# The statistics of the first four tiles of a fused block, shared out anew between VectorE, ScalarE and GpSimd

## The chip, the core and the metric

The kernel runs on one core of one Trainium2 chip. The metric is the device time of one execution in microseconds; the median of seven runs of the kernel before is 174.38 us.

## What is computed

The input x has 2048 rows (tokens) of 448 columns. It is normalized once, and two branches work on the normalized rows: an attention with a softmax feature map, and a token-shifting MLP. The sum of x and both branches is the output.

```
def _layernorm(x, eps=1e-5):
    m = mean(x, axis=-1); v = var(x, axis=-1)
    return (x - m) / sqrt(v + eps)

xn = _layernorm(x)
# A: qkv = xn @ wqkv; phi = softmax feature map of q, k by w_phi; linear attention; @ wo
# B: h = gelu(_layernorm(xn) @ w1), shifted by tokens in four groups of columns, @ w2; x1 = xn + that
#    x1 + gelu(_layernorm(x1) @ w3) @ w4
out = x + A(xn) + B(xn)
```

The change concerns only the first line of that, the normalization of x, and of it only the first four of sixteen tiles.

## The kernel before

**Tiles.** A tile is 128 rows. `xtok` holds the sixteen tiles of x, `xn` the normalized ones in 512 columns, `xnT` their transposes, which nearly all matmuls read. Per tile, `st`, `mv` and `rs` hold eight float32 columns each: raw statistics, mean and variance, and the reciprocal root.

**Who sets the order.** The order is written out by hand. A recorder keeps the instructions in program order; each engine runs its own in that order, and a semaphore is waited for wherever a tile was written by another engine. So an instruction that waits holds up everything behind it on its engine. `play` runs a list of steps that stand in the wanted order.

**Loads.** The loads are issued at the start. SyncE's queue has tile 0, tile 2, tile 3, the second half of `wv`, tiles 4 and 5, tiles 6 and 7, `w1`, then the rest; ScalarE's queue has tile 1 and the first half of `wv`, and then loads an activation table.

**Head, tiles 0 to 3.** `ln1_two(i)` does two tiles: for each, VectorE takes the statistics (`ln_stats`: a statistics instruction over 448 columns and an aggregate that gives mean and variance), and ScalarE takes the square root of variance plus epsilon (`epsb` holds the epsilon); then for each, VectorE takes the reciprocal and applies mean and factor (`ln1_apply`, one instruction over 512 columns with the two halves overlapping). It is called for tiles 0 and 1, and then for 2 and 3. From tile 4 on, `ln1_stats` does the statistics on VectorE and lets GpSimd add epsilon and raise to the power of -1/2 (`ln_scale`, with `mhalf` holding -0.5).

`xn_T(i, b)` transposes a tile by eight TensorE instructions into the bank pair b, from where ScalarE copies it into `xnT` (from tile 10 on in part VectorE). `spin(n, 256)` is n matmuls on dummy data, which keep TensorE busy while it waits.

**The first matmuls.** `V(i, 0)` and `V(i, 1)` are the two parts of `v_pair(i, b)`, the product of tiles i and i + 1 with `wv`, eight matmuls and six; `row_pairs` issues them in pairs, one on the lower and one on the upper 64 partitions. `WA` and `WC` are products with `w1`, `FO` folds `w_phi` into the query and key weights, `v_out` copies a V result out of the bank (ScalarE). The list begins:

```
ln1_two(0)
spin(19, 256)
play([(xn_T, 0, 0), (spin, 3, 256), (xn_T, 1, 1)])
ln1_two(2)
...
play([(spin, 4, 256), V(0, 0), (xn_T, 2, 0), V(0, 1), (xn_T, 3, 1),
      (spin, 2, 256), V(2, 0), (v_out, 0, 2), (tables, "gelu_apprx_tanh_and_others"), WA(0, 0), (xn_T, 4, 1),
      V(2, 1), (v_out, 2, 3), (xn_T, 5, 2), WA(0, 1), WC(0, 0), (xn_T, 6, 3), WC(0, 1), (wc_out, 0, 1),
```

ScalarE has the table with the square root loaded at first, and the one with the gelu between the copy of V(0) and the first gelu. Behind this stage come the folds, the attention's feature maps, the shifted product with `w2`, and the long stage of `w3`, `w4` and `wo`, all of them as before.

Of the kernel before, what the change touches and what calls it, by code (L numbers as in the profile page):

```python
# [5 lines left out]
ACT = mybir.ActivationFunctionType  # L6
ALU = mybir.AluOpType
AX = mybir.AxisListType
BF16 = mybir.dt.bfloat16
F32 = mybir.dt.float32  # L10

LN_EPS = 1e-5
# [208 lines left out]
def bass_parallel_sum__linear_kernel_hedgehog__mixer_s_mlp__prompt_kernel(  # L221
    nc, A_x, A_wqkv, A_w_phi, A_wo, B_x, B_w1, B_w2, B_w3, B_w4, out,
):
    _, S, D = A_x.shape
# [3 lines left out]
    NT, NG, KC, NC, NM, FC, HP = 16, 4, 4, 4, 4, 14, 32  # L228
# [7 lines left out]
    with es:  # L236
        R = Recorder(nc, es)
        total = [0]

        def region(name, nbytes):  # L240
            nbytes = -(-nbytes // 64) * 64
            total[0] += nbytes
            h = es.enter_context(nc.sbuf_tensor(name, [128, nbytes // 2], BF16))
            R.track(h, nbytes)
            return h

        def view(h, cols, dt=BF16, at=0):
            a = h[:, at // 2:at // 2 + cols * DTB[dt] // 2]
            return a if dt == BF16 else a.bitcast(dt)

        def new(name, cols, dt=BF16):
            return view(region(name, cols * DTB[dt]), cols, dt)
# [6 lines left out]
        banks = [pairs[b // 2][:, 512 * (b % 2):512 * (b % 2) + 512] for b in range(8)]  # L259


        xtok = new("xtok", NT * D).rearrange("p (t d) -> p t d", t=NT)
        xn = new("xn", NT * 512).rearrange("p (t d) -> p t d", t=NT)
        xnT_r = region("xnT", KC * S * 2)
        xnT = view(xnT_r, KC * S).rearrange("p (c s) -> p c s", c=KC)
# [11 lines left out]
        wv = new("wv", KC * D).rearrange("p (c d) -> p c d", c=KC)  # L277
# [20 lines left out]
        st = new("st", NT * 8, F32).rearrange("p (t c) -> p t c", t=NT)  # L298
        mv = new("mv", NT * 8, F32).rearrange("p (t c) -> p t c", t=NT)
        rs = new("rs", NT * 8, F32).rearrange("p (t c) -> p t c", t=NT)  # L300
# [3 lines left out]
        ksum = new("ksum", 4 * 32, F32).rearrange("p (b c) -> p b c", b=4)  # L304
        rks = new("rks", 4 * 32, F32).rearrange("p (b c) -> p b c", b=4)
        mhalf = new("mhalf", 8, F32)
        epsb = new("epsb", 8, F32)

        h3T = view(phik_r, 2 * FC * 512).rearrange("p (b c f) -> p b c f", b=2, c=FC)
        oT = view(xnT_r, 2 * KC * 512).rearrange("p (b c s) -> p b c s", b=2, c=KC)  # L310
# [30 lines left out]
        dve, pool = "DVE", "POOL"  # L341
# [43 lines left out]
        def tables(name):  # L385
            R.op("ACT", lambda e: e.preload_act_table_set(name), [], [])

        tables("sqrt_and_others")
        R.ew(pool, "memset", ident[:, :], 0.0)
        R.op(pool, lambda e: e.affine_select(ident[:, :], ident[:, :], pattern=[[-1, 128]],  # L390
                                             compare_op=ALU.not_equal, fill=1.0, base=0, channel_multiplier=1),
# [4 lines left out]
        R.ew(pool, "memset", hD[:, :, 512:DW], 0.0)  # L396
        busy = gT[:, 0, 0, 0:256]
        R.ew(dve, "memset", busy, 1.0)
        R.ew(dve, "memset", epsb[:, :], LN_EPS)
        R.ew(dve, "memset", vp[:, :, DH + 1:HP], 0.0)  # L400
        R.ew(dve, "memset", vp[:, :, DH:DH + 1], 1.0)
        mb = maskb[0:CR, :].rearrange("p (h e) -> p h e", h=4)
# [27 lines left out]
        def lap(a):  # L430
            return bass.AP(a.tensor, a.offset, [list(a.ap[0]), [192, 2], [1, 256]])

        def halves(a):
            return a.rearrange("p (b e) -> p b e", b=2)

        def ln_stats(stt, mvt, src, i):
            R.ew(dve, "bn_stats", stt[:, i, 0:6], src[:, i, 0:D])
            R.ew(dve, "bn_aggr", mvt[:, i, 0:2], stt[:, i, 0:6])
# [8 lines left out]
        def ln_apply(eng, dst, src, mvt, rst, i):  # L447
            m, op = (mvt[:, i, 0:1], ALU.subtract) if eng == dve else (rst[:, i, 1:2], ALU.add)
            R.ew(eng, "tensor_scalar", dst, src, m, rst[:, i, 0:1], op0=op, op1=ALU.mult)
# [6 lines left out]
        def ln1_apply(eng, i):  # L456
            ln_apply(eng, halves(xn[:, i, :]), lap(xtok[:, i, :]), mv, rs, i)
# [3 lines left out]
        def spin(n, cols):  # L461
            for _ in range(n):
                R.mm(banks[7][:, 0:cols], busy[:, 0:128], busy[:, 0:cols], True, True)
# [49 lines left out]
        LO, HI = (0, 64), (64, 128)  # L513

        def row_pairs(first, second, start=False, cols=1):
            for s, (p, q) in enumerate(zip(first, second)):
                for out, lhs, rhs in (p, q) if cols == 1 else (*p, *q):
                    R.mm(out, lhs, rhs, start and s == 0, False)

        def lap_pair(outs, lhs, rhs):  # L520
            def side(k, rows, kcs):
                return [(outs[k], lhs(k, kc, *rows), rhs(k, kc, *rows)) for kc in kcs]
            return (lambda: row_pairs(side(0, LO, (0, 1, 2, 3)), side(1, HI, (0, 1, 2, 3)), True),
                    lambda: row_pairs(side(1, LO, (0, 1, 3)), side(0, HI, (0, 2, 3))))

        def k_pair(i, b):
            return lap_pair([banks[2 * b + k][:, 0:D] for k in range(2)],
                            lambda k, kc, lo, hi: xnT[lo:hi, kc, 128 * (i + k):128 * (i + k) + 128],
                            lambda k, kc, lo, hi: wpk[lo:hi, kc, :])

        def q_pair(g, c, b):
            return lap_pair([banks[2 * b + k] for k in range(2)],
                            lambda k, kc, lo, hi: wpq[lo:hi, kc, 128 * (c + k):128 * (c + k) + 128],
                            lambda k, kc, lo, hi: xnT[lo:hi, kc, 512 * g:512 * g + 512])

        def v_pair(i, b):
            return lap_pair([banks[2 * b + k][:, 0:D] for k in range(2)],
                            lambda k, kc, lo, hi: xnT[lo:hi, kc, 128 * (i + k):128 * (i + k) + 128],
                            lambda k, kc, lo, hi: wv[lo:hi, kc, :])

        def v_out(i, b, eng="ACT"):
            vd = vaug[:, i:i + 2, :].rearrange("p t (h e) -> p t h e", e=HP)[:, :, :, 0:DH]
# [237 lines left out]
        def play(fs):  # L780
            for f in fs:
                f[0](*f[1:])

        def ln1_two(i):
            for j in (i, i + 1):
                ln_stats(st, mv, xtok, j)
                R.act(rs[:, j, 1:2], mv[:, j, 1:2], ACT.Sqrt, bias=epsb[:, 0:1])
            for j in (i, i + 1):
                R.ew(dve, "reciprocal", rs[:, j, 0:1], rs[:, j, 1:2])
                ln1_apply(dve, j)  # L790

        ln1_two(0)
        spin(19, 256)
        play([(xn_T, 0, 0), (spin, 3, 256), (xn_T, 1, 1)])
        ln1_two(2)
        for i in range(4, 10):
            ln1_stats(i, 1, 0)
            if i > 4:
# [10 lines left out]
        def ln1_end():  # L809
# [5 lines left out]
            late_3()  # L815

        vps = {i: v_pair(i, b) for i, b in ((0, 2), (2, 3), (4, 2), (6, 3), (8, 2), (10, 2), (14, 3))}
        was = {g: wa_pair(g, b) for g, b in ((0, 0), (1, 0), (2, 0), (3, 3))}
        wcs = {g: wc_pair(g, b) for g, b in ((0, 1), (1, 1), (2, 0), (3, 0))}
# [3 lines left out]
        def V(i, k):  # L823
            return (vps[i][k],)

        def WA(g, k):
            return (was[g][k],)

        def WC(g, k):
            return (wcs[g][k],)  # L830
# [4 lines left out]
        def FO(t, m, k):  # L835
            return (fps[t, m][k],)

        play([(spin, 4, 256), V(0, 0), (xn_T, 2, 0), V(0, 1), (xn_T, 3, 1),
              (spin, 2, 256), V(2, 0), (v_out, 0, 2), (tables, "gelu_apprx_tanh_and_others"), WA(0, 0), (xn_T, 4, 1),
              V(2, 1), (v_out, 2, 3), (xn_T, 5, 2), WA(0, 1), WC(0, 0), (xn_T, 6, 3), WC(0, 1), (wc_out, 0, 1),  # L840
              V(4, 0), (xn_T, 7, 3), (wa_out, 0, 0), V(4, 1), (v_out, 4, 2), V(6, 0),
              WC(1, 0), V(6, 1), (v_out, 6, 3), WA(1, 0), (xn_T, 8, 2, 2), WC(1, 1), (wc_out, 1, 1), WA(1, 1), (wa_out, 1, 0),
# [19 lines left out]
        side = [12, 0, 1, 2, 3, 8, 9, 10]  # L862
        for ps in range(8):
            k, q = k_pair(2 * ps, 1), q_pair(ps // 2, 2 * (ps % 2), 0)
            w = (w2_pair if ps else v_pair)(side[ps], 2)
            if not ps:
                play([(k[0],), (w[0],), (k[1],), (k_exp, 0, 1, 0), (k_exp, 0, 1, 1), (q[0],), (w[1],), (v_out, 12, 2, "DVE"),
# [117 lines left out]
```

The softmax here doesn't subtract the row's maximum and nothing guards it: scores larger than these inputs give would overflow.

## Time and profile before

| what | value |
|---|---|
| median of 7 runs | 174.38 us (174.19 to 175.06) |
| the profiled execution's own time | 174.38 us |
| its span in the profile | 172.7 us |
| TensorE busy, share of the span | 168.7 us, 98% |
| VectorE, ScalarE, GpSimd busy | 114.3, 84.4, 88.8 us |
| first transposes (tile 0) start | 5.39 us |
| first WA matmul starts | 10.15 us |
| starts of the applies of tiles 0, 1, 2, 3 | 4.92, 5.44, 7.42, 7.94 us |
| starts of ScalarE's copies of tiles 0, 1, 2, 3 | 5.72, 6.38, 8.22, 8.92 us |
| second table load of ScalarE | 10.34 us, for 1.28 us |

The times inside are counted from the start of the span. A line of the timeline gives start, duration, engine, source line, operation, what is written and read, and the shape; a bracket at its end tells how long the engine was idle before it and who ended that. Nearly all instructions are recorded by a helper, so the source line is the helper's (L200 matmuls, L204 transposes, L208 ScalarE, L212 elementwise), and the tiles' names tell which step it is. In the profile, DVE is VectorE, ACT ScalarE, POOL GpSimd, PE TensorE, and PEld its weight loads.

### The profile page before, as it was taken

How to read it: one execution, taken by the hardware profiler on the slowest of the kernel's cores; microseconds unless marked ns; L12 is line 12 of the kernel's file. 1: busy time of each engine (PE TensorE's matmuls, PEld its weight loads, DVE VectorE, ACT ScalarE, POOL GpSimd, SP SyncE). 2: the span in 40 equal slices, each digit the busy share in tenths (PEclk: the TensorE clock that was granted, in tenths of full speed). 3: DMA queues.
4: the chain of work that ended last, by engine and by line, in shares of the span. 5: the costliest groups of instructions: out<-in, count | busy, mean ns of one | idle time of the engine just before them, and what ended most of it. 6: DMA issues, size and time to landing. Idle time of an engine off the chain costs nothing.

```text
span 172.7 us, 5218 instructions
## 1 busy us (share of the span) xinstructions
PE 168.7 (98%) x2272; PEld 91.5 (53%) x2272; DVE 114.3 (66%) x263; ACT 84.4 (49%) x99; POOL 88.8 (51%) x123
## 2 busy tenths in 40 slices
PE   7999999999999999999999999999999999999994
PEld 5565576544555554554555555545545555545553
DVE  4999975277999999976577962445417425474621
ACT  3599874988778877947225322224204222224000
POOL 3065570015789999930639389440720714522740
DMA  5995552139942011044103932034411220311331
GB/s 164 327 212 91 113 125 55 44 45 366 382 151 47 19 30 30 4 37 89 33 1 65 91 63 60 28 87 93 93 30 55 61 57 4 84 30 34 84 86 55
DMA packets 32679, 15.21 MB, mean 88 GB/s; under 512 B 23952, under 2 KB 32016, under 8 KB 32656
## 3 DMA queue, kind: packets, MB, share of 16 engines
q1 hardware_dynamic: 32096, 14.51, 36.5%
q8 instruction: 18, 0.29, 0.8%
q10 hardware_dynamic: 560, 0.37, 0.7%
q14 instruction: 5, 0.04, 0.1%
HBM read 7.14 MB, written 1.84 MB: 52 GB/s over the span
## 4 chain that ended last, share of the span: by engine, by line
PE 95%; DVE 2%; issue 1%; ACT 0%
PE bank L200 94%; PE bank L204 1%; DVE vaug L212 1%; DVE st L212 1%; ACT xnT L208 0%; DVE xn L212 0%; DVE mv L212 0%; DVE gT L212 0%; DVE rs L212 0%; DVE epsb L212 0%
## 5 line engine op out<-in xcount | busy, mean ns | idle before, releaser
L208 ACT ACTIVATE phik<-bank 128x1024 bf16<-128x1024 f32 (+1 forms) x44 | 42.3, 984 | 60.5 <-PE bank L200 60.5
L200 PE MATMUL bank<-gT,w 64*128 64x512 bf16 x392 | 50.2, 377 | 0.1
L212 DVE TENSOR_TENSOR vaug<-bank,vaug 128x464 f32<-128x464 f32 (+3 forms) x65 | 32.7, 512 | 22.5 <-PE bank L200 20.9
L200 PE MATMUL bank<-w,phik 64*128 64x448 bf16 (+3 forms) x434 | 45.2, 343 | 0.0
L212 POOL TENSOR_TENSOR xnT<-vaug 128x196 bf16<-128x196 f32 (+1 forms) x32 | 18.1, 587 | 46.6 <-DVE vaug L212 46.6
L200 PEld LDWEIGHTS bank<-w,phik 64*128 64x128 bf16 (+1 forms) x434 | 22.9, 94 | 20.3 <-issue 0.4
L212 POOL TENSOR_TENSOR phik<-phik,rks 128x1792 bf16<-128x1792 bf16 x8 | 25.6, 3214 | 10.4 <-DVE rks L212 10.3
L200 PEld LDWEIGHTS bank<-gT,w 64*128 64x128 bf16 x392 | 17.8, 94 | 17.6 <-issue 0.6
L212 POOL TENSOR_TENSOR vaug<-xn,xtok 128x448 f32<-128x448 bf16 x16 | 16.2, 1033 | 0.2 <-DVE vaug L212 0.2
L212 DVE RECIPROCAL vaug<-bank 128x16 f32<-128x16 f32 x16 | 4.1, 257 | 18.2 <-PE bank L200 18.2
L212 DVE TENSOR_REDUCE ksum<-phik 128x64 f32<-128x1792 bf16 x8 | 16.1, 2010 | 0.0
L200 PE MATMUL bank<-xnT,wpq 64*128 64x512 bf16 x112 | 14.7, 376 | 0.0
L200 PE MATMUL bank<-wv,xnT 64*128 64x448 bf16 x112 | 13.9, 351 | 0.1
L200 PE MATMUL bank<-wo,xnT 64*128 64x448 bf16 (+3 forms) x110 | 13.6, 343 | 0.0
L200 PE MATMUL bank<-xnT,w 64*128 64x512 bf16 (+2 forms) x168 | 13.4, 306 | 0.0
L200 PE MATMUL bank<-w,hT 64*128 64x448 bf16 x112 | 13.2, 349 | 0.0
L200 PE MATMUL bank<-wpk,xnT 64*128 64x448 bf16 x112 | 13.2, 349 | 0.0
L212 POOL TENSOR_TENSOR rs<-mv,mhalf 128x1 f32<-128x1 f32 (+2 forms) x16 | 10.8, 676 | 1.3
L212 DVE TENSOR_TENSOR xn<-bank,xn 128x512 bf16<-128x512 f32 (+1 forms) x16 | 9.2, 620 | 3.1 <-PE bank L200 3.1
L212 DVE BATCH_NORM_STATS2 st<-xtok 128x6 f32<-128x448 bf16 x16 | 9.8, 613 | 0.0
L212 POOL TENSOR_SCALAR mv<-mv 128x1 f32<-128x1 f32 (+2 forms) x16 | 3.8, 239 | 11.2 <-DVE mv L212 10.7
L212 POOL TENSOR_SCALAR g_tok<-xn,rs 128x512 bf16<-128x512 bf16 x12 | 9.1, 772 | 0.3
(67 smaller groups left out, 173.6 us busy)
## 6 DMA issues: line engine op xcount, KB each, us to landing
w<-in_B_w_dram SPq DMA_DIRECT2D x2, 896.0 KB, 5.8
out_dram<-vaug SPq DMA_DIRECT2D x15, 112.0 KB, 1.9
w<-in_B_w_dram SPq DMA_DIRECT2D x1, 1568.0 KB, 11.4
xtok<-in_A_x_dram SPq DMA_DIRECT2D x2, 448.0 KB, 6.3
xtok<-in_A_x_dram SPq DMA_DIRECT2D x2, 224.0 KB, 4.9
w<-in_B_w_dram SPq DMA_DIRECT2D x2, 224.0 KB, 5.1
wo<-in_A_wo_dram SPq DMA_DIRECT2D x2, 224.0 KB, 6.9
xtok<-in_A_x_dram SPq DMA_DIRECT2D x3, 112.0 KB, 2.8
```

The costliest lines, as they stand in the source:

```text
L200: self.op("PE", lambda e: e.matmul(out, lhsT, rhs, start=start, stop=stop, skip_group_check=True), [out], [lhsT, rhs], tile=self._tile(lhsT))
L204: self.op("PE", lambda e: e.transpose(out, in_, ident), [out], [in_, ident], tile=self._tile(in_))
L208: self.op("ACT", lambda e: e.activation(out, in_, func, **kw), [out], [in_] + aps)
L212: self.op(eng, lambda e: getattr(e, name)(out, *args, **kw), [out], aps)
```

## The change

The square root on ScalarE goes for tiles 0 to 3, and with it the square root table, the second table load and `epsb`; the gelu table is loaded at the start. Statistics of tiles 0, 2 and 3 stay on VectorE, which now also adds epsilon to the variance by a one-column instruction; the power of -1/2 comes from GpSimd. Tile 1's statistics come from ScalarE in two passes over its 448 columns that also add up what they write: one of x/448 (the mean) and one of x²/448. VectorE squares the mean and takes epsilon from it, GpSimd subtracts this from the mean of the squares and raises to the power. The passes write their unused columns into `xn` of tiles 15 and 14.

VectorE's order becomes: statistics of tile 0 with epsilon, squared mean of tile 1, statistics of tile 2 with epsilon, apply of tile 0, statistics of tile 3 with epsilon, applies of tiles 1, 2 and 3. GpSimd's is: power of tile 0, subtraction and power of tile 1, powers of tiles 2 and 3.

The first part of `v_pair` is split: for tiles 0 to 3, `V(i, 0)` has the four matmuls of the first two column blocks and `V(i, 2)` the four of the others, with the transposes of tile 3 between them at V(0); tile 2's transposes come ahead of V(0, 0). There are 19 + 5 + 1 + 2 spins in place of 19 + 3 + 4 + 2. After the first WA the order on TensorE is the old one.

```
-        tables("sqrt_and_others")
+        tables("gelu_apprx_tanh_and_others")
...
-        R.ew(dve, "memset", epsb[:, :], LN_EPS)
...
         def v_pair(i, b):
+            def side(k, rows, kcs):
+                lo, hi = rows
+                return [(banks[2 * b + k][:, 0:D], xnT[lo:hi, kc, 128 * (i + k):128 * (i + k) + 128], wv[lo:hi, kc, :])
+                        for kc in kcs]
+
+            def early():
+                row_pairs(side(0, LO, (0, 1)), side(1, HI, (0, 1)), True)
+                if i > 3:
+                    mid()
+
+            def mid():
+                row_pairs(side(0, LO, (2, 3)), side(1, HI, (2, 3)))
+            return early, lambda: row_pairs(side(1, LO, (0, 1, 3)), side(0, HI, (0, 2, 3))), mid
...
-        def ln1_two(i):
-            for j in (i, i + 1):
-                ln_stats(st, mv, xtok, j)
-                R.act(rs[:, j, 1:2], mv[:, j, 1:2], ACT.Sqrt, bias=epsb[:, 0:1])
-            for j in (i, i + 1):
-                R.ew(dve, "reciprocal", rs[:, j, 0:1], rs[:, j, 1:2])
-                ln1_apply(dve, j)
-
-        ln1_two(0)
+        def ln1_pow(j, at):
+            R.ew(pool, "tensor_tensor", rs[:, j, 0:1], mv[:, j, at:at + 1], mhalf[:, 0:1], op=ALU.pow)
+
+        def ln1_one(j):
+            ln_stats(st, mv, xtok, j)
+            R.ew(dve, "tensor_scalar", mv[:, j, 2:3], mv[:, j, 1:2], LN_EPS, 1.0, op0=ALU.add, op1=ALU.mult)
+            ln1_pow(j, 2)
+
+        def ln1_sum(j, func, scale, to):
+            out, in_, acc = xn[:, NT - 1 - to // 3, 0:D], xtok[:, j, :], mv[:, j, to:to + 1]
+            R.op("ACT", lambda e: e.activation(out, in_, func, scale=scale, accum_out=acc), [out, acc], [in_])
+
+        ln1_sum(1, ACT.Copy, 1.0 / D, 0)
+        ln1_sum(1, ACT.Square, D ** -0.5, 3)
+        ln1_one(0)
+        R.ew(dve, "tensor_scalar", mv[:, 1, 2:3], mv[:, 1, 0:1], mv[:, 1, 0:1], -LN_EPS, op0=ALU.mult, op1=ALU.add)
+        R.ew(pool, "tensor_tensor", mv[:, 1, 4:5], mv[:, 1, 3:4], mv[:, 1, 2:3], op=ALU.subtract)
+        ln1_pow(1, 4)
+        ln1_one(2)
+        ln1_apply(dve, 0)
+        ln1_one(3)
+        ln1_apply(dve, 1)
         spin(19, 256)
-        play([(xn_T, 0, 0), (spin, 3, 256), (xn_T, 1, 1)])
-        ln1_two(2)
+        play([(xn_T, 0, 0), (spin, 5, 256), (xn_T, 1, 1)])
+        ln1_apply(dve, 2)
+        ln1_apply(dve, 3)
...
-        play([(spin, 4, 256), V(0, 0), (xn_T, 2, 0), V(0, 1), (xn_T, 3, 1),
-              (spin, 2, 256), V(2, 0), (v_out, 0, 2), (tables, "gelu_apprx_tanh_and_others"), WA(0, 0), (xn_T, 4, 1),
+        play([(spin, 1, 256), (xn_T, 2, 0), (spin, 2, 256), V(0, 0), (xn_T, 3, 1), V(0, 2), V(0, 1),
+              V(2, 0), V(2, 2), (v_out, 0, 2), WA(0, 0), (xn_T, 4, 1),
```

More of the change, by code (lines that the diff above doesn't have):

```diff
@@ L306, in bass_parallel_sum__linear_kernel_hedgehog__mixer_s_mlp__prompt_kernel @@
         mhalf = new("mhalf", 8, F32)
-        epsb = new("epsb", 8, F32)
         h3T = view(phik_r, 2 * FC * 512).rearrange("p (b c f) -> p b c f", b=2, c=FC)
@@ L536, in v_pair @@
         def v_pair(i, b):
-            return lap_pair([banks[2 * b + k][:, 0:D] for k in range(2)],
-                            lambda k, kc, lo, hi: xnT[lo:hi, kc, 128 * (i + k):128 * (i + k) + 128],
-                            lambda k, kc, lo, hi: wv[lo:hi, kc, :])
+            def side(k, rows, kcs):
[9 more added lines that the diff above has]
+            return early, lambda: row_pairs(side(1, LO, (0, 1, 3)), side(0, HI, (0, 2, 3))), mid
         def v_out(i, b, eng="ACT"):
```

## The prediction

> **What bounds the kernel now.** First the page's busy rows and its chain.
>
> ```profile
> span 172.7 us, 5218 instructions
> PE 168.7 (98%) x2272; PEld 91.5 (53%) x2272; DVE 114.3 (66%) x263; ACT 84.4 (49%) x99; POOL 88.8 (51%) x123
> PE 95%; DVE 2%; issue 1%; ACT 0%
> ```
>
> TensorE is the bound almost throughout. The change touches no matmul of the body, so it can win or lose only by moving the moment from which TensorE runs without a gap. The chain in order of time gives that moment.
>
> ```profile
> 3.46 0.45 DVE st L212
> ...
> 4.92 0.42 DVE xn L212
> ...
> 5.39 0.29 PE bank L204 x8
> ...
> 8.92 0.61 ACT xnT L208
> ...
> 9.57 1.63 PE bank L200 x15
> ```
>
> To 5.39 us the chain is VectorE's statistics, then it alternates; its last step outside TensorE is ScalarE's copy of tile 3 at 8.92. From 9.57 on it is matmuls. I take as landmark the first WA matmul, which starts at 10.15: the same matmuls stand before it in both kernels (14 of V(0), 8 of V(2), transposes of tiles 0 to 3). VectorE's timeline gives the durations.
>
> ```profile
> 3.27 0.63 DVE L212 BATCH_NORM_STATS2 st<-xtok 128x6 f32<-128x448 bf16 x1
> 3.93 0.18 DVE L212 BATCH_NORM_AGGREGATE mv<-st 128x2 f32<-128x6 f32 x1
> 4.03 0.59 DVE L212 BATCH_NORM_STATS2 st<-xtok 128x6 f32<-128x448 bf16 x1
> 4.66 0.18 DVE L212 BATCH_NORM_AGGREGATE mv<-st 128x2 f32<-128x6 f32 x1
> 4.75 0.13 DVE L212 RECIPROCAL rs<-rs 128x1 f32<-128x1 f32 x1
> 4.92 0.41 DVE L212 TENSOR_SCALAR xn<-xtok,mv,rs 128x512 bf16<-128x512 bf16 x1
> 5.25 0.15 DVE L212 RECIPROCAL rs<-rs 128x1 f32<-128x1 f32 x1
> ```
>
> Start to start: statistics to aggregate 0.66; aggregate to an independent instruction 0.10, to one that needs it 0.18 + 0.04 = 0.22; a one-column step 0.10 to what needs nothing of it; an apply 0.33.
>
> **The change, part by part. VectorE's new order.** Starting at 3.27 as before (the landing of tile 0 decides that, so the lost epsilon memset gives nothing): statistics of tile 0 3.27, aggregate 3.93, epsilon 4.15, square of tile 1's mean 4.25, statistics of tile 2 4.35, aggregate 5.01, epsilon 5.23, apply of tile 0 5.33 (before 4.92), statistics of tile 3 5.66, aggregate 6.32, epsilon 6.54, apply of tile 1 6.64 (before 5.44), of tile 2 6.97 (7.42), of tile 3 7.30 (7.94), statistics of tile 4 at some 7.7 (8.27). One statistics step, one aggregate and four reciprocals go; four one-column steps come. VectorE leads by 0.5 us afterwards, but tile 1 is 1.2 us later, since its apply now stands behind all of tile 3's statistics.
>
> **Landing of tile 3.** That instruction also waits for a DMA. The DMA rows of the moment when it is issued (1.72), and of the three loads of one tile together:
>
> ```profile
> xtok<-in_A_x_dram SPq DMA_DIRECT2D x1, 112.0 KB, 4.2
> xtok<-in_A_x_dram SPq DMA_DIRECT2D x3, 112.0 KB, 2.8
> ```
>
> It landed at 1.72 + 4.2 = 5.92; its neighbour of the same size took 2.8, which would be 4.5. Before, tile 3 was wanted at 6.52 only, so this was covered; after, it is wanted at 5.66, and as traced it adds 5.95 - 5.66 = 0.29. Both ends stay: 0 and 0.29.
>
> **ScalarE's two passes.** No accumulating pass is in the trace. Copies of 512 columns take 0.60 and of 896 take 0.91, so 448 take 0.55; at most I add a one-column activation (0.29) for reading the sum, 0.84. Tile 1 lands at 0.82 + 2.6 = 3.42, so the mean is there at 4.0 to 4.3 (wanted by VectorE at 4.25: 0 to 0.09 late) and the squares at 4.6 to 5.1. I take the lower price, nearest to the rows of the same operation. Queued behind them is only the copy of tile 0's transposes, due at about 6.1.
>
> **GpSimd's powers.** Its rows:
>
> ```profile
> 9.20 0.19 POOL L212 TENSOR_SCALAR mv<-mv 128x1 f32<-128x1 f32 x1 [6.54 <-DVE mv L212]
> 9.47 0.57 POOL L212 TENSOR_TENSOR rs<-mv,mhalf 128x1 f32<-128x1 f32 x1
> 12.39 0.34 POOL L212 TENSOR_SCALAR mv<-mv 128x1 f32<-128x1 f32 x1 [0.16 <-DVE mv L212]
> ```
>
> From the end of VectorE's step to GpSimd 0.09, the power 0.57, back 0.04. Tile 0: 4.28 + 0.70 = 4.98, wanted at 5.33. Tile 1: subtraction (0.19 to 0.34) from about 5.1, power until some 6.1, wanted at 6.64. Tile 2 until some 6.8, wanted at 6.97. Tile 3: 6.67 + 0.70 = 7.37, a 0.07 wait, hidden because its transposes queue until 8.5. Covers of 0.35, 0.5, 0.2: I cost the powers at nothing; were tile 1's power the later one, its excess over 0.5 would go straight into the sum.
> The row of 0.34 is a GpSimd step that started beside a VectorE apply (12.27 to 12.68); alone it takes 0.19. [...]
>
> **TensorE.** An apply's end to its transposes takes 0.06 (5.33 to 5.39), those to ScalarE's copy 0.33 (6.05 to 6.38), the copy 0.60, and 0.06 to the matmul. Tile 1: apply ends 7.05, transposes 7.11, copy 7.44 to 8.04, second matmul of V(0,0) 8.09 (before 7.03). Then no wait is left: rest of V(0,0) 0.38, transposes 0.13 (7.89 to 8.02), four matmuls of V(0,2) 0.38, six of V(0,1) 0.58 (8.02 to 8.60), eight of V(2) 0.76 (13.64 to 14.40): WA at 10.32. Tile 3's copy, at about 9.4, is in time. That is 0.17 late, or 0.46 with tile 3 as traced. The split of V(0,0) is what lets tile 3's transposes in early and removes the old stall at 9.13; the spins (9 become 8) lie in waits and cost nothing.
>
> **The table load.** 1.28 us of ScalarE at 10.34 goes; it was followed by the next activation 0.01 later, and delayed the copy of tile 4 and a wait of tile 6's transposes at 12.98: at most 0.04 of that wait isn't TensorE's own pace. [...]
>
> **Sum.** Behind 10.15 the body follows TensorE's own order: a wait for VectorE's casts at 24.5 (0.2) would absorb lag, but the next wait, for ScalarE at 26.6 (0.25), hangs on transposes that lag too, so nothing is given back. +0.17 - 0.04 = +0.13, with tile 3 as traced +0.42; the middle, as neither landing row is nearer, is +0.27. The profiled execution's own time is 174.38 (span 172.7 and 1.7 around it), equal to the median of the seven runs. Forecast 174.65.
>
> **Rivals.** Slower: tile 3's landing ends the chain later than traced. It decides from about 5.95; the second half of wv, issued 0.47 later, landed at 6.9, and a landing at 6.6 gives +1.1, 175.45. For it: a load of 4.2 us beside 2.8 shows that landings scatter, and the cover of 0.6 is gone; against: nothing in the loads changes.
> Faster: VectorE's lead of 0.5 and the freed ScalarE shorten the waits behind 10.15 (0.14 at 12.98, 0.2 at 24.5, 0.25 at 26.6) while tile 3 is early: 0.13 - 0.5 gives 174.0. Against: these waits sit in TensorE's own loops.
> Not doing what it says: passes of over 1.3 us each would make tile 1's power the last thing (over 6.64) and its statistics slower than VectorE's; the rows at 0.55 speak against. It would give 174.9 and more.
> TensorE's clock: it ran at half speed (0.21 between spins) until 4.6, and the new head idles more between 5.2 and 8.1. No row shows a fall back; half speed over 3.4 us, the time that it took to rise, would cost up to 1.7.
>
> **How the numbers follow.** 0.2% is 0.35 us, about what a measurement of this kernel can tell from no change. The forecast, +0.1 to +0.35, has 0.43. Tile 3 as traced or later 0.32, slow passes 0.05 and the clock 0.05 make slower 0.42; faster 0.15. The range leaves out the deep end of the faster case and landings after some 6.6 with most of the clock case: 174.1 to 175.4.
>
> **What would show it.** Right: applies of tiles 0 and 1 at 5.3 and 6.6 to 6.9, tile 3's statistics begin with its landing or at 5.7, WA at 10.3 to 10.6, no stall at V(2,0). Wrong: WA before 10.1; a power that VectorE waits for by over 0.1 at tiles 0 to 2; a spacing of 0.2 between spins after 5; a lag that shrinks between 10 and 31.

## The result and the profile after

The changed kernel takes 176.00 us (median of 13 executions, 174.66 to 176.70), the kernel before 174.45 (34 executions, 174.03 to 175.12). The ratio is 1.0075, interval 1.0055 to 1.0095. The forecast was 174.65, with a range to 175.4: the sign held, the size did not. The times of the changed kernel fall into two heaps: four between 174.66 and 174.95, near the forecast, and nine between 175.61 and 176.70. The profiled execution (176.14, span 174.4) is of the second heap.

The page and the chain of the changed kernel, against those of before:

```profile
span 174.4 us, 5216 instructions
PE 170.0 (97%) x2271; PEld 91.4 (52%) x2271; DVE 114.0 (65%) x260; ACT 83.4 (48%) x98; POOL 91.5 (52%) x128
```

```profile
3.50 1.24 ACT xn L802 x4
...
4.77 0.21 DVE mv L212
...
5.92 0.33 DVE xn L212
...
6.30 0.40 PE bank L204 x8
6.69 1.18 PE bank L200 x5
7.87 0.33 PE bank L204 x8
```

TensorE has a matmul less and is busy 1.3 us longer. The chain now runs through ScalarE's two passes (L802) and VectorE's squared mean, and tile 0's transposes come at 6.30, not 5.39. The timeline of TensorE shows the larger thing:

```profile
1.25 4.23 PE L200 MATMUL bank<-gT 128*128 128x256 bf16 x19 [1.25 <-DVE gT L212]
6.30 0.40 PE L204 MATMUL bank<-ident,xn 64*128 64x64 bf16 x8 [0.81 <-DVE xn L212]
6.63 1.25 PE L200 MATMUL bank<-gT 128*128 128x256 bf16 x5
7.80 0.40 PE L204 MATMUL bank<-ident,xn 64*128 64x64 bf16 x8
8.13 0.39 PE L200 MATMUL bank<-gT 128*128 128x256 bf16 x1
8.46 0.40 PE L204 MATMUL bank<-ident,xn 64*128 64x64 bf16 x8
...
10.04 0.42 PE L204 MATMUL bank<-ident,xn 64*128 64x64 bf16 x8
10.28 2.25 PE L200 MATMUL bank<-wv,xnT 64*128 64x448 bf16 x18
12.36 1.03 PE L200 MATMUL bank<-xnT,w 64*128 64x512 bf16 x8
13.23 0.28 PE L204 MATMUL bank<-ident,xn 64*128 64x64 bf16 x8
```

Eight transposes take 0.40 to 0.42 until 10 us and 0.28 at 13; before, they took 0.29 already at 5.39. Five spins take 1.25, spaced by 0.21. TensorE worked at half clock until it rose between 10.3 and 11.0 (within the line of eighteen, the spacing of a pair falls from 0.33 to 0.19). In the profile of before it rose between 4.6 and 4.8, within the nineteen spins. Between 5.49, the end of the last spin, and 6.30 TensorE stood idle for 0.81 us. The first WA comes at 12.36, 2.2 late.

### The profile page after: what moved, and what is told of

The parts are those of the page before. It is cut to its first block, busy times and chain, and to the rows that moved or that the text cites. A ratio compares the mean times of both kernels' runs of the same rounds, so it can differ in the third digit from the quotient of the medians.

```text
span 174.4 us, 5216 instructions
## 1 busy us (share of the span) xinstructions
PE 170.0 (97%) x2271; PEld 91.4 (52%) x2271; DVE 114.0 (65%) x260; ACT 83.4 (48%) x98; POOL 91.5 (52%) x128
## 4 chain that ended last, share of the span: by engine, by line
PE 95%; DMA 2%; DVE 1%; ACT 1%; issue 0%
PE bank L200 94%; DMA xtok<-in_A_x_dram 2%; PE bank L204 1%; ACT xn L802 1%; DVE mv L212 0%; DVE st L212 0%; DVE xn L212 0%; DVE vaug L212 0%
## 5 line engine op out<-in xcount | busy, mean ns | idle before, releaser
L212 POOL TENSOR_TENSOR phik<-phik,rks 128x1792 bf16<-128x1792 bf16 x8 | 25.6, 3216 | 10.4 <-DVE rks L212 10.3
L212 POOL TENSOR_TENSOR rs<-mv,mhalf 128x1 f32<-128x1 f32 (+2 forms) x20 | 13.2, 661 | 3.9 <-DVE mv L212 2.4
L208 ACT ACTIVATE xnT<-bank 128x512 bf16<-128x512 bf16 x12 | 6.9, 596 | 5.3 <-PE bank L204 5.1
L212 DVE BATCH_NORM_STATS2 st<-xn 128x6 f32<-128x448 bf16 x16 | 9.2, 577 | 0.0
```

Source lines behind the costliest of these rows:

```text
L208: self.op("ACT", lambda e: e.activation(out, in_, func, **kw), [out], [in_] + aps)
L212: self.op(eng, lambda e: getattr(e, name)(out, *args, **kw), [out], aps)
```

## The experiments

Theory A: half clock lasts until TensorE has been busy for some 3.4 us without a long gap (an estimate from the profile of before, where the spins began at 1.26 and the clock rose between 4.6 and 4.8), the idle 0.81 us broke that stretch, and this is most of the loss. Theory B: the loss is the later first tiles, and the clock is an accident of the profiled execution.

**The gap filled.** The changed kernel, otherwise untouched:

```
-        spin(19, 256)
+        spin(23, 256)
```

> Changed kernel with 23 spins instead of 19 ahead of tile 0's transposes, nothing else. Theory A (the clock): TensorE stood idle from 5.5 to 6.3 us in the changed kernel, its clock therefore stayed at half until 10.6, and that is most of the loss; with the gap filled (4 spins at 0.213 = 0.85) the clock rises before 8.1 in every run: median 174.5 to 175.0, no run over 175.5. Theory B (the later tile 1 alone, the clock a thing of this one profile): the spins change nothing, median 175.8 to 176.2 and the same spread from 174.7 to 176.7.

174.88 us, 174.63 to 175.40 in twelve executions, ratio to before 1.0014 (1.0001 to 1.0027). The second heap is gone. Its timeline of TensorE:

```profile
6.36 0.29 PE L204 MATMUL bank<-ident,xn 64*128 64x64 bf16 x8 [0.57 <-DVE xn L212]
6.58 0.72 PE L200 MATMUL bank<-gT 128*128 128x256 bf16 x5
```

Tile 0 is as late as before (6.36), but transposes take 0.29 and five spins 0.72: full clock, risen at about 5. Only spins were added, so the statistics can't explain the difference: theory B falls. Of the 0.75% that the change cost, filling the gap gives back 0.61%, or 1.07 us; 0.14%, or 0.24 us, stays. These are ratios over all executions. Between the two profiled executions more stays, 0.6 us (span 173.3 against 172.7), so the smaller part is known only roughly.

**The gap alone, in the kernel before.**

```
-        spin(19, 256)
+        spin(15, 256)
```

> Kernel before with 15 spins instead of 19, so that TensorE stands idle from about 4.7 to 5.4 us; the statistics, tables and the order of the work are the old ones. Theory A: some runs keep half clock until 8 or more: times spread from 174.2 up to 175.5 or 176, median up by 0.3 or more. Theory B: 174.45, spread 174.0 to 175.1, as before.

175.31 us, 174.12 to 176.82; six of twelve executions lie at 175.71 or more, five of eleven without the longest. The ratio is 1.0035 (1.0007 to 1.0062), wide because it mixes two heaps. The old statistics, four spins fewer, and the same picture:

```profile
5.47 0.40 PE L204 MATMUL bank<-ident,xn 64*128 64x64 bf16 x8 [0.83 <-DVE xn L212]
5.79 0.82 PE L200 MATMUL bank<-gT 128*128 128x256 bf16 x3
6.55 0.40 PE L204 MATMUL bank<-ident,xn 64*128 64x64 bf16 x8
6.88 1.03 PE L200 MATMUL bank<-gT 128*128 128x256 bf16 x4
7.84 1.43 PE L200 MATMUL bank<-wv,xnT 64*128 64x448 bf16 x8
9.11 0.28 PE L204 MATMUL bank<-ident,xn 64*128 64x64 bf16 x8
```

The gap is 0.83, half clock lasts past 7.8, and this execution took 175.75. That is theory A from the other side.

**Half of the gap.**

```
-        spin(19, 256)
+        spin(17, 256)
```

> Kernel before with 17 spins instead of 19: at half clock TensorE stands idle for some 0.35 us ahead of tile 0's transposes, about half of the gap with 15 spins (which gave 175.31, six of twelve runs over 175.7). Theory A, with a gap of 0.35 enough to break a stretch: as with 15 spins, several runs over 175.7. If only a longer gap breaks it: as with 19 spins, 174.0 to 175.3, median 174.6.

174.70 us, 174.38 to 175.15, ratio 1.0008 (0.9993 to 1.0023): as with 19 spins. In its profile TensorE waits 0.42 for tile 0 (5.01 to 5.43) and works at full clock behind it; the clock had risen at the end of the spins there, so it is the twelve times that speak. At half clock, by the spacing of 0.21, the spins would end at about 5.07, an estimated gap of 0.36. Not every gap matters: one of about 0.4 was forgiven in all twelve, 0.83 in half of the executions was not. The sharper form of theory A in the expectation was wrong.

**The needless wait.** In the changed kernel VectorE stops ahead of the squared mean:

```profile
4.21 0.15 DVE L212 TENSOR_SCALAR mv<-mv 128x1 f32<-128x1 f32 x1
4.77 0.21 DVE L212 TENSOR_SCALAR mv<-mv 128x1 f32<-128x1 f32 x1 [0.40 <-ACT xn L802]
```

It needs only the first pass, but starts when the second has ended:

```profile
3.50 0.58 ACT L802 ACTIVATE xn<-xtok 128x448 bf16<-128x448 bf16 x1 [0.49 <-DMA xtok<-in_A_x_dram]
3.99 0.19 ACT L802 ACTIVATION_READ_ACCUMULATOR xn<-xtok 128x1 f32 x1
4.08 0.56 ACT L802 ACTIVATE xn<-xtok 128x448 bf16<-128x448 bf16 x1
4.55 0.19 ACT L802 ACTIVATION_READ_ACCUMULATOR xn<-xtok 128x1 f32 x1
```

The first sum is there at 4.18, the second at 4.74. The recorder follows writes in grains of 32 bytes (`GRAIN`), and a tile's eight columns of `mv` are one grain; mean and mean of squares count as one thing. The experiment gives the second sum another buffer:

```
-            out, in_, acc = xn[:, NT - 1 - to // 3, 0:D], xtok[:, j, :], mv[:, j, to:to + 1]
+            out, in_, acc = xn[:, NT - 1 - to // 3, 0:D], xtok[:, j, :], (st2 if to else mv)[:, j, to:to + 1]
...
-        R.ew(pool, "tensor_tensor", mv[:, 1, 4:5], mv[:, 1, 3:4], mv[:, 1, 2:3], op=ALU.subtract)
+        R.ew(pool, "tensor_tensor", mv[:, 1, 4:5], st2[:, 1, 3:4], mv[:, 1, 2:3], op=ALU.subtract)
```

> Changed kernel with the sum of squares written into another buffer, so that VectorE's square of the mean waits for the first ScalarE pass and not for both (4.77 in the changed kernel's profile, where the first sum was ready at 4.2). Both theories: squared mean at 4.3, apply of tile 0 at 5.4 instead of 5.84, tile 1 at 6.7 instead of 7.1. Theory A: the idle gap shrinks from 0.8 to 0.4, so fewer runs keep half clock: median 174.4 to 175.3, runs with full clock 174.3 to 174.6. Theory B: 0.4 earlier everywhere, 175.6.

VectorE of this kernel:

```profile
4.18 0.28 DVE L212 TENSOR_SCALAR mv<-mv 128x1 f32<-128x1 f32 x2
...
5.31 0.41 DVE L212 TENSOR_SCALAR xn<-xtok,mv,rs 128x512 bf16<-128x512 bf16 x1
5.63 0.62 DVE L212 BATCH_NORM_STATS2 st<-xtok 128x6 f32<-128x448 bf16 x1
...
6.58 1.26 DVE L212 TENSOR_SCALAR xn<-xtok,mv,rs 128x512 bf16<-128x512 bf16 x3
```

The two small steps run together, and the applies start at 5.31, 6.58, 6.89 and 7.42, where the prediction's sum had put them (5.33, 6.64, 6.97, about 7.4). The median is 174.71 (174.27 to 175.23, and one execution of 176.82), ratio 1.0011 (0.9987 to 1.0035). The idle stretch ahead of tile 0 is 0.29 and the clock rose at 5.9 in its profile, still within the head: WA at 10.47.

That is still 0.15 later than the sum's 10.32. V(0, 1) now follows V(0, 2) at once, and its first weight load waits for TensorE's own matmuls:

```profile
8.53 1.35 PE L200 MATMUL bank<-wv,xnT 64*128 64x448 bf16 x10
9.13 0.49 PEld L200 LDWEIGHTS bank<-wv,xnT 64*128 64x128 bf16 x8 [0.50 <-PE bank L200]
```

From the last pair of V(0, 2) to the first of V(0, 1) it is 0.42 (8.72 to 9.14) where two pairs are otherwise 0.19 apart, and 0.41 to 0.42 in the profiles of all six kernels with the split. The kernel before has the same 0.41 between V(0, 0) and V(0, 1) (7.61 to 8.02), but there tile 2's transposes stand in it. So the new order leaves some 0.2 uncovered.

**Both repairs.** The second buffer and 21 spins:

> Changed kernel with both repairs: the sum of squares in its own buffer, and 21 spins instead of 19, which at half clock reach to 5.9, past the transposes of tile 0 at 5.8. Theory A (half clock lasts until TensorE has been busy without a gap for some 3.4 us): no gap of 0.3 or more ahead of the first rise, so every run has full clock by 8.1: median 174.3 to 174.7, none over 175.3 (the same kernel with 19 spins had 174.71 and one run of 176.82). Rival C (the rise is chance, gaps of this size don't matter once the statistics are early): as with 19 spins, single runs of 176 and more remain.

174.72 us, 174.07 to 175.14 and one execution of 175.86; ratio 1.0011 (0.9992 to 1.0030). The median lies just above theory A's expected range, and the single long execution is nearly what rival C named: this doesn't exclude that something beside the gap delays the rise now and then. In its profile WA starts at 10.40.

**The powers without ScalarE's passes.** One part of the change alone in the kernel before: gelu table from the start, epsilon on VectorE, powers on GpSimd, but tile 1's statistics on VectorE and the matmuls in their old order:

```
+        ln1_one(0)
+        ln1_one(1)
+        ln1_apply(dve, 0)
+        ln1_one(2)
+        ln1_apply(dve, 1)
...
+        ln1_one(3)
+        ln1_apply(dve, 2)
+        ln1_apply(dve, 3)
```

> Kernel before with one part of the change alone: no square root table, epsilon by VectorE, powers by GpSimd for tiles 0 to 3, but tile 1's statistics stay on VectorE and the matmuls keep their order. By the changed kernel's durations: applies at 5.25, 6.55, 7.9, 8.6 (before 4.92, 5.44, 7.42, 7.94), WA at 10.7 to 10.8 with full clock. Theory A: idle from 5.2 to 5.7 lets some runs keep half clock: median 174.9 to 175.8, spread over 1.2. Theory B: lag of 0.6 alone, 175.0, spread as before.

175.23 us, 174.82 to 175.64, ratio 1.0030 (1.0015 to 1.0045). Applies at 5.16, 6.42, 7.68 and 8.53, WA at 10.98. There is no second heap: the median lies within theory A's range and 0.2 over theory B's, but the small spread is as B had it. The gap that theory A counted on was hardly there: in the profile the spins end at 5.48 and tile 0's transposes start at 5.62, so this kernel doesn't test the clock. The profile is accounted for by a lag of 0.83 at WA and 0.7 in the span (173.4 against 172.7), so here the later applies are the cost. This kernel has no ScalarE table load in the middle either, and at most 0.04 of its lag was given back by tile 6's transposes (13.98 against 13.18): the load was hidden, as predicted.

**Tile 1's apply first.** Both repairs, and:

```
-        ln1_one(3)
         ln1_apply(dve, 1)
+        ln1_one(3)
```

> The kernel with both repairs, and tile 1's apply ahead of tile 3's statistics. Tile 1's power is there at 5.95, so the apply comes at about 6.0 instead of 6.6, VectorE waits 0.3 for it, and tile 3's apply comes at 7.9 to 8.0 instead of 7.4. If tile 1's place behind tile 3's statistics costs what the prediction put on it, the first WA matmul comes 0.3 to 0.4 earlier than with both repairs alone, at 10.0 to 10.2 with full clock, and the median is 174.0 to 174.4; if the end is set elsewhere, 174.3 to 174.7 as without it.

174.51 us, 174.30 to 174.78, ratio 0.9993 (0.9981 to 1.0005): no difference from the kernel before, and the narrowest spread of all. The earlier apply did not shorten the path: tile 1's transposes came only 0.1 earlier than with both repairs (6.86 against 6.97), and WA at 10.51. TensorE shows why:

```profile
6.86 0.29 PE L204 MATMUL bank<-ident,xn 64*128 64x64 bf16 x8
7.08 0.28 PE L200 MATMUL bank<-gT 128*128 128x256 bf16 x1
7.52 0.29 PE L204 MATMUL bank<-ident,xn 64*128 64x64 bf16 x8 [0.15 <-DVE xn L212]
7.74 0.39 PE L200 MATMUL bank<-gT 128*128 128x256 bf16 x2
8.07 0.55 PE L200 MATMUL bank<-wv,xnT 64*128 64x448 bf16 x4
```

Tile 1's apply, from 5.79 to 6.20, was no longer what ended the chain: the five spins behind tile 0's transposes held tile 1's back until 6.86, in an execution whose clock rose at 6.3, against 5.4 with both repairs alone. Then tile 2's wait for their apply, and two spins follow ahead of V(0,0).

**Without those spins.**

```
-        play([(spin, 1, 256), (xn_T, 2, 0), (spin, 2, 256), V(0, 0),
+        play([(xn_T, 2, 0), V(0, 0),
```

> The kernel with both repairs and tile 1's apply first, without the three spins around tile 2's transposes. There the first V(0) matmuls started at 8.07, behind two spins, although the copy of tile 1 that they need ended at 7.8. If those spins lie on the path, V(0) starts at 7.85, tile 3's transposes (apply 7.90, so 8.37) come next, WA at 10.2 instead of 10.5, and the median falls by 0.2 to 0.3, to 174.2 to 174.4. If the half clock is still decided behind 6 us, the missing spins open gaps of 0.4 at most, which were harmless in the kernel before with 17 spins: no run over 175.3. Rival: those gaps do break the stretch, and single runs come to 175.5 and more.

174.52 us, 174.32 to 175.03, ratio 1.0005 (0.9992 to 1.0018). The gain did not come. In the profiled execution the clock rose only at 7.2, so tile 1's transposes came at 7.32 and WA at 10.74; whether the three spins cost anything at an equal moment of the rise is left open. No execution was over 175.3, as expected for small gaps. No version was clearly faster than the kernel before.

**The record of the clock.** The changed kernel's trace has the granted clock from 10.58 us on, full for 163.840 us and then half; that of the kernel before has no entry. The profile's clock row reads full speed in the head of both, and the half clock there is read from the spacing of the matmuls: spins 0.21 apart and eight transposes in 0.40 at half clock, 0.11 and 0.29 at full. Estimated in this way, the clock rose at 5.9 in the kernel with its own buffer (transposes at 5.78 in 0.31), 6.4 with the powers alone (three spins from 5.95 in 0.70), and in the three kernels with 21 spins, in the order in which they stand above, at 5.4 (the 21 spins in 4.50, where the other two took 4.66), 6.3 and 7.2 (five spins behind tile 0's transposes in 0.75 and in 1.21). The rise did not come at a fixed time from the start: the two kernels with tile 1's apply first are the same up to tile 1's transposes, and rose at 6.3 and 7.2.

So a fixed 3.4 us, as theory A has it, is not shown: the three kernels with 21 spins have no gap ahead of tile 0, and their clock rose 4.1, 5.0 and 6.0 us after the first spin at 1.25. What the profiles do show is that the long gap goes with a late rise. With one of 0.81 (5.49 to 6.30) the clock rose at 10.58, 4.3 behind the gap's end; with one of 0.29 (5.49 to 5.78) it rose at 5.9, 0.1 behind it. Why the same kernel falls now into one heap and now into the other, these traces don't tell.

## Why the prediction was wrong, and where it was right

**Bound and landmark.** Right that all is decided by the moment from which TensorE runs without gaps. The landmark flattered the kernel before by up to 0.19: its first WA, 10.15, was that of the lower half, with the upper half's V(2,0) still a matmul behind after the stall at 9.13; the changed kernel starts both halves together. This is in the 0.2 that the changed kernel's lag loses from WA (2.21) to tile 6's transposes (15.18 against 13.18). "Then no wait is left" missed one: the 0.2 between V(0, 2) and V(0, 1).

**VectorE's order and the landing.** Durations and order were right: the kernel with its own buffer matched every apply within 0.1. Tile 3 was in time: its statistics started straight behind tile 0's apply, at 6.16 in the changed kernel and at 5.63 in the one with its own buffer. Its load, issued at 1.72, took 3.1 and 3.6 in these two and landed at about 4.8 and 5.3. The landing at 5.92 didn't recur, so its 0.29 (0.15 of it in the forecast), and the slower rival built on it, weren't needed.

**ScalarE's passes: the first step that failed.** The size was right: the sum was ready 0.68 after a pass began, within 0.55 to 0.84. But "0 to 0.09 late" took for granted that VectorE waits for the first pass alone. It waited for both, 4.77 instead of 4.25, and everything behind came 0.5 later: tile 0's apply at 5.84 instead of 5.33, and the gap grew to 0.81. The diff doesn't show this; the grain in the recorder's code does.

**GpSimd's powers.** Right at nothing: no apply of tiles 0 to 2 waited for a power. Tile 3's power started at 7.26 beside the apply of tile 1, took 0.65 where tile 0's took 0.56, and tile 3's apply came at 7.95, 0.1 behind the end of tile 2's (7.83).

**TensorE: the second step that failed, and the dear one.** "The spins lie in waits and cost nothing", and the whole count of TensorE at 0.19 a pair, took the rise at 4.6 as given, as if it were tied to the work and not to what the spins keep up. The rival on the clock asked whether a risen clock might fall back, put half speed over 3.4 us at 1.7 us, and gave it 0.05; what happened is that it rose too late, at 10.58 in the profile, and nine of the thirteen executions are about as long as that one. One of the prediction's own signs of being wrong came true with it: spins spaced by 0.2 after 5 us. The price was of the right order (1.07 us by the ratios, 0.61%), the chance was far off. The rows to see it were there: by the prediction's own sum tile 0's transposes come at 5.80, and nineteen spins at half clock end at 5.49, so a gap of 0.3 opens in the only stretch in which the clock was known to be rising. That gap alone does little, as the kernel with its own buffer shows (1.0011), though one of its twelve executions took 176.82. The needless wait made it 0.81. So the first failed step is what the second was paid for, and undoing either, the wait (1.0011) or the gap (1.0014), takes most of the loss away. Without long gaps the rise came between 4.6 and 7.2, that is 3.4 to 6.0 us after the first spin at 1.25; with the gap of 0.8 it came at 10.58 in the changed kernel's profile, 9.3 after it.

**Table load and what lies behind.** The load was worth 0.04 at most, as said. "Nothing is given back" holds roughly: beside the 0.2 above, the changed kernel's lag falls by 0.08 until 31 us.

**The rest.** With the gap filled, the change costs 0.24 us by the ratio; the forecast had +0.27. That agreement is luck. Errors of opposite sign stand behind it: 0.59 for the needless wait (WA at 11.06 with the gap filled, at 10.47 with its own buffer) and 0.2 for the wait between V(0, 2) and V(0, 1), against the 0.15 for tile 3's landing and the 0.2 of the landmark. From 0.27 they lead to about 0.7, which is the lag of the profiled execution with 23 spins at tile 6's transposes (13.87 against 13.18); why the ratio is smaller is open.

**Open.** Single executions of 176.82 and 175.86, in kernels with a gap of 0.3 and with none ahead of tile 0, have no profile. Where between 0.42 and 0.81 a gap begins to matter was not tried. The new order of the first matmuls was not run by itself. Between 31 and 94 us profiled executions of the eight tried kernels gain or lose up to 0.35 on the one before, in both directions; this was not followed.

## What to carry to other kernels

Dummy matmuls at the head of a kernel are part of its timing: if a change delays the first real work, count the idle time that opens behind them, and price a late rise of the clock (1.07 us here) before any of the microseconds on the other engines. Where two results of one engine are consumed apart, give them separate grains of whatever tracks the dependencies; which instruction a wait stands for has to be read in the tracker. A spread that falls into heaps is a finding of its own; one profile belongs to one of them.

## What the runs showed of the hardware that was not expected

An idle stretch of 0.8 us while the clock was still halved cost over 1 us in the median (176.00 against 174.88); one of about 0.4 us cost nothing that twelve executions show. The moment of the clock's rise varied between profiled executions with the same head: about 6.3 and 7.2 us in the two kernels with tile 1's apply first. A ScalarE instruction with an accumulating output is two in the trace: 0.58 for 448 columns and 0.19 for reading the accumulator, of which 0.1 overlaps, so that two passes follow each other by 0.58.
